# Spatial-reduction attention and a mixture of adapters on one core: a new start (load order, idle products on TensorE, new order list for the first 14 slots)

## The chip, the cores and the metric

The kernel runs on 1 core of one Trainium2 chip. The metric is the device time of one execution in microseconds. Before the change it is 393.75 us, the median of 4 runs (393.65 to 394.62).

## The reference

Queries `q` (4 batches, 12288 tokens each, 128 channels), `kv` (4 batches, 384 x 32 positions, 128 channels) and small weights, all fp32. Each batch pools `kv` by 4 x 4 positions to 768 rows and multiplies them with `w_sr`; the result serves as keys and as values. Softmax attention of all queries over these 768 keys gives `x`, and a mixture of 8 low-rank adapters (2 of 8 by token) adds to it:

```python
kv_pool = kv.reshape(B, H // 4, 4, W // 4, 4, C).mean(axis=(2, 4))
k = v = kv_pool.reshape(B, -1, C) @ w_sr
a = softmax(q @ k.T / sqrt(C));  x = a @ v
logits = x @ w_gate              # the two largest of 8, softmax over the two
out = x + sum over the two: weight * (x @ A[e]) @ B[e]
```

## The kernel before

The 49152 tokens are cut into 96 slots of 512 (24 for each batch; four slots are a query group). For each slot TensorE does three score pairs (two products of 512 columns each, PSUM tile `sg`, two buffers), ScalarE takes the exponential of each pair (`em`, line 252), TensorE multiplies `em` with the values in 24 products of 137 columns (`acc`, one buffer: 128 channels, 8 gate logits, and the row sum), VectorE normalizes (`xn`, lines 264 and 268), and the adapters follow: transposes (`tt_ps`), down product (`h_ps`), gate (`hg`), transposes, up product (`d_ps`), and the sum that goes out (`osb`). The routing (lines 299 to 314) runs on GpSimd, for slots 0 and 1 on VectorE.

The small PSUM tiles share a pool of two buffers (`mb`). All instructions are kept in the order in which they are written for their engine. This order comes from a list of short items that `follow` reads, for the first 14 slots and for the last 24 slots by hand; for slots 14 to 71 `slot(k)` writes it. The items that matter here, with their arguments:

- `sc k r`: score pair r (of 3) of slot k, and its exponential; `at k s`: 6 of the 24 attend products of slot k; `nm k`: its normalization.
- `tq g m E`: query turn, four fp32 transposes of one chunk of query group g and the copy to `qT` on engine E (A is ScalarE, V is VectorE). Groups 0 and 1 are loaded in fp32 and turned like this; later groups are cast to bf16 by a GpSimd DMA (`cast_q`) and read back through a DMA transpose on SP's queue (`lq`, `load_qT`).
- `ad h i`: one of four pair sums of key block h (of 3) of batch 0 on VectorE (line 175): two of the four rows of a pooling window are added. `ky h half`: 8 fp32 transposes ("key turns") that add up in PSUM; then the mean (line 206). `k2 h`: projection of the keys (line 213). `va h`: projection of the values (line 222).
- `cs1`: the GpSimd instruction that reads the last column of query group 1 and thereby holds the two first casts behind that load; `kv b h r`: a load of batch b. `pa` and `pr`: sums on GpSimd and preparation of the next batch.

Ahead of the list stand the loads on SP's queue: query group 0 as one DMA of 1 MB, the 24 pieces of 256 KB of the three key blocks of batch 0, four pieces of query group 1, and the adapters' weights. `w_sr` and `w_gate` come by ScalarE's queue; VectorE and TensorE then make `wext` and its gate part from them.

Of the kernel before, what the change touches and what calls it, by code (L numbers as in the profile page):

```python
# [20 lines left out]
def kernel(  # L21
# [10 lines left out]
    nc = tc.nc  # L32
# [74 lines left out]
    def turn_q(g, m, engine):  # L107
        if g not in qT:
            qT[g] = qpool.tile([P, GT], BF16, tag="qT", name="qT")
        ps = mtile([P, S, P], name="qT_ps")  # L110
        for i in range(S):
            mm(ps[:, i], q_f[g][:, m * S + i], id_f, is_transpose=True,
               start=(i == 0), stop=(i == S - 1))
        o = qT[g][:, m * T:(m + 1) * T].rearrange("p (s t) -> p s t", s=S)
        if engine is nc.scalar:
            keep(nc.scalar.copy(o, ps))
        else:
            keep(nc.vector.tensor_copy(o, ps))
# [6 lines left out]
    load_q(0, 0, GC * S)  # L125
    for h in range(3):
        for r in range(4):
            for x in range(2):
                load_kv(0, h, r, x)
    for m in range(GC):  # L130
        load_q(1, m * S, m * S + S)
    b_f = const.tile([P, C], FP32)
    keep(nc.sync.dma_start(b_f, moe_B.rearrange("e r c -> (e r) c")))
    a_f = const.tile([P, P], FP32)
    keep(nc.sync.dma_start(a_f, moe_A.rearrange("e c r -> c e r")))


    warm = const.tile([P, 1], FP32)
    nc.vector.memset(warm, 0.0)
    keep(nc.scalar.activation(warm, warm, AF.Exp, bias=0.0, scale=1.0))  # L140
    id_f = const.tile([P, P], FP32)
    make_identity(nc, id_f)
    id_bf = const.tile([P, P], BF16)
    nc.vector.tensor_copy(id_bf, id_f)
    wext = const.tile([P, VC], FP32)
    nc.vector.tensor_copy(wext[:, 0:C], w_sr_sb)
    wT_ps = mtile([P, C], name="wT_ps")
    mm(wT_ps, w_sr_sb, id_f, is_transpose=True, start=True, stop=True)
    wT = const.tile([P, C], FP32)
    nc.vector.tensor_copy(wT, wT_ps)  # L150
    w2_ps = mtile([P, E], name="w2_ps")
    mm(w2_ps, wT, w_gate_sb, start=True, stop=True)
    nc.vector.tensor_copy(wext[:, C:VC], w2_ps)


    kfT, vx = {}, {}

    def prepare(b, adder):
# [3 lines left out]
        def pool_step(h, step, lo, hi):  # L162
            t = kvr[b, h]
            if step < 3:
                u, v = t[:, 0].rearrange("p g c -> p (g c)"), t[:, step + 1].rearrange("p g c -> p (g c)")
            else:
                w = 2 * C if step == 3 else C
                u, v = t[:, 0, :, 0:w], t[:, 0, :, w:2 * w]
                keep(adder.tensor_tensor(u, u, v, op=ALU.add))
                return  # L170
            keep(adder.tensor_tensor(u[:, lo:hi], u[:, lo:hi], v[:, lo:hi], op=ALU.add))  # L171

        def pair_step(h, r, x):
            u, v = (kvr[b, h][:, r + i, x] for i in range(2))
            keep(adder.tensor_tensor(u, u, v, op=ALU.add))

        for h in range(3):
            if adder is nc.vector:
                sums.append([lambda h=h, r=r, x=x: pair_step(h, r, x)
                             for r in (0, 2) for x in range(2)])  # L180
                continue
# [5 lines left out]
        def keys(h, half=None):  # L187
            if h == 0 and half != 1:
                st["kpT"] = prep.tile([P, J, P], FP32, tag="kpT", name="kpT")
                kfT[b] = per_b.tile([P, J, P], BF16, tag="kfT", name="kfT")  # L190
            kpT = st["kpT"]
            if half != 1:
                st["ps"] = mtile([P, 2, P], name="kpT_ps")
            ps = st["ps"]
            if adder is nc.vector:
                parts = [(r, i, c) for r in (0, 2) for i in range(2) for c in range(4)]
            else:
                parts = [(0, i, 0) for i in range(2)]
            for n, (r, i, c) in enumerate(parts):
                if half is not None and r // 2 != half:  # L200
                    continue
                mm(ps[:, i], kvr[b, h][:, r, i, c * C:(c + 1) * C], id_f, is_transpose=True,
                   start=(n == 0), stop=(n == len(parts) - 1))
            if half == 0:
                return
            keep(nc.vector.tensor_scalar(kpT[:, 2 * h:2 * h + 2], ps, 1.0 / 16.0, None,
                                         op0=ALU.mult))

        def keys2(h):
            kpT = st["kpT"]  # L210
            ps = mtile([P, 2, P], name="kfT_ps")
            mm(ps, w_sr_sb, kpT[:, 2 * h:2 * h + 2], start=True, stop=True)
            keep(nc.vector.tensor_copy(kfT[b][:, 2 * h:2 * h + 2], ps))  # L213

        def values(h):
# [7 lines left out]
            if adder is not nc.vector:  # L223
                st["vb", h] = prep.tile([P, 2, C], BF16, tag="vb", name="vb")
                keep(nc.vector.tensor_copy(st["vb", h], ps[:, :, 0:C]))
# [8 lines left out]
        for h in range(3):  # L234
            for f in (keys, keys2, values) if adder is nc.vector else (keys, values, turn):
                rest.append(lambda h=h, f=f, **how: f(h, **how))
# [17 lines left out]
    def attend(k, s):  # L254
        b = k // NB
        if k not in acc:
            acc[k] = ps_a.tile([P, S, 256], FP32, tag="acc", name="acc")
        o = acc[k][:, s, 0:VE]
        for j in range(J):
            mm(o, em[k][:, j, s * P:(s + 1) * P], vx[b][:, j], start=(j == 0), stop=(j == J - 1))  # L260
# [11 lines left out]


# [16 lines left out]
    def route(k0):  # L290
        n = size[k0] * S
        eng = nc.gpsimd if k0 > 1 else nc.vector
# [74 lines left out]
    def bank(pool):  # L367
# [20 lines left out]
    def turn_x(k, pool):  # L388
        xT[k] = quad(bank(pool).bitcast(BF16), pool)
        xb = xn[k].bitcast(U16)[:, :, 1::2].bitcast(BF16)  # L390
        for s in range(S):
            mm(xT[k][:, s // 2, s % 2], xb[:, s, 0:C], id_bf, is_transpose=True,
               start=(s % 2 == 0), stop=(s % 2 == 1))

    def copy(engine, o, i):
        keep(nc.scalar.copy(o, i) if engine == "A" else nc.vector.tensor_copy(o, i))  # L396

    def fetch_x(k, engine):
        sb = run.tile([P, S, P], BF16, tag="tt1", name="tt1")
        copy(engine, four(sb), xT[k])  # L400
        xT[k] = sb
# [3 lines left out]
    def hold_h(k, pool):  # L405
        hps[k] = quad(bank(pool).bitcast(BF16), pool)

    def turn_h(k, lo=0, hi=S):
        for s in range(lo, hi):
            mm(hps[k][:, s // 2, s % 2], hg[k][:, s], id_bf, is_transpose=True,  # L410
               start=(s % 2 == 0), stop=(s % 2 == 1))

    def fetch_h(k, lo=0, hi=S, engine="A"):
        if lo == 0:
            hgT[k] = run.tile([P, S, P], BF16, tag="tt1", name="tt1")
        copy(engine, part(four(hgT[k]), lo, hi), part(hps[k], lo, hi))

    def hold_acc(k, pool="sg"):
        acc[k] = bank(pool)
# [3 lines left out]
    def attend_part(k, lo, hi):  # L423
        for s in range(S):
            for j in range(lo, hi):
                mm(acc[k][:, s, 0:VE], em[k][:, j, s * P:(s + 1) * P], vx[k // NB][:, j],
                   start=(j == 0 and s % 2 == 0), stop=(j == J - 1 and s % 2 == 1))

    def down_into(k, pool):
        hp[k] = quad(bank(pool), pool)  # L430
        for s in range(S):
            mm(hp[k][:, s // 2, s % 2], xT[k][:, s], a_bf, start=(s % 2 == 0), stop=(s % 2 == 1))

    def gate_part(k, lo, hi):
        if lo == 0:
# [3 lines left out]
        keep(nc.vector.tensor_tensor(  # L439
            part(four(hg[k]).rearrange("p a b (e r) -> p a (b e) r", e=E), lo, hi),  # L440
            part(four(hp[k]).rearrange("p a b (e r) -> p a (b e) r", e=E), lo, hi),
            part(g4, lo, hi).unsqueeze(3).broadcast_to([P, (hi - lo) // 2, 2 * E, RK]), op=ALU.mult))

    def hold_d(k, pool):
        dp[k] = quad(bank(pool), pool)

    def up_part(k, lo, hi):
        for s in range(lo, hi):
            mm(dp[k][:, s // 2, s % 2], hgT[k][:, s], b_bf, start=(s % 2 == 0), stop=(s % 2 == 1))
# [5 lines left out]
    def add_here(k, lo, hi, queue="SP"):  # L455
        osb = opool.tile([P, S, C], FP32, tag="osb", name="osb")[:, 0:hi - lo]
        keep(nc.vector.tensor_tensor(osb.rearrange("p (a b) c -> p a b c", b=2),
                                     part(four(dp[k]), lo, hi),
                                     part(four(xn[k][:, :, 0:C]), lo, hi), op=ALU.add))
# [57 lines left out]
    def plan(b):  # L517
        if b not in plans:
            plans[b] = prepare(b, nc.gpsimd if b else nc.vector)
# [3 lines left out]
        "tq": lambda g, m, e: turn_q(g, m, nc.scalar if e == "A" else nc.vector),  # L523
        "ad": lambda h, i: plan(0)[0][h][i](),
        "ky": lambda h, half: plan(0)[1][3 * h](half=half),
        "k2": lambda h: plan(0)[1][3 * h + 1](),
        "va": lambda h: plan(0)[1][3 * h + 2](),
        "cs": lambda: first_casts(kvr[0, 2][:, 3, 1, 0:1]),
        "cs1": lambda: first_casts(q_f[1][:, GC * S - 1, 0:1]),
# [10 lines left out]
        "xt": turn_x, "cx": lambda k, e="A": fetch_x(k, e), "hb": hold_h, "ht": turn_h, "ch": fetch_h,  # L540
        "o95": hold_acc, "pt": attend_part, "dn2": down_into, "ge2": gate_part,
# [4 lines left out]
    def follow(order):  # L546
        for item in order.replace("\n", " ").split(";"):
            what, *at = item.split()
# [31 lines left out]
ad 0 0; tq 0 0 A; ad 0 1; ad 0 2; cs1; tq 0 1 A; ad 0 3; ky 0 0; tq 0 2 V; ky 0 1; k2 0; ad 1 0; va  # L580
0; sc 0 0; tq 0 3 A; lq 2; sc 2 0; ad 1 1; ad 1 2; ad 1 3; ky 1 0; sc 1 0; ky 1 1; ad 2 0; sc 3 0;
k2 1; ad 2 1; va 1; sc 3 1; ad 2 2; sc 0 1; ky 2 0; sc 2 1; ad 2 3; kv 1 0 0; ky 2 1; sc 1 1; k2 2;
tq 1 0 V; sc 0 2; va 2; cab; sc 4 2; tq 1 1 V; at 0 2; kv 1 0 1; sc 1 2; at 0 1; sc 4 0; at 0 0; at
# [89 lines left out]
```

## Time and profile before

| | |
|---|---|
| median of 4 runs | 393.75 us |
| profiled execution, its own time | 393.65 us |
| its span, first to last instruction | 391.9 us |
| TensorE busy | 377.0 us (96%) |
| VectorE busy | 324.8 us (83%) |
| ScalarE busy | 298.1 us (76%) |
| GpSimd busy | 204.7 us (52%) |
| DMA | 76.47 MB, mean 195 GB/s |
| chain that ended last | TensorE 93%, VectorE 3%, DMA 1%, issue 1%, ScalarE 1% |

Busy times overlap. A product that is listed with 379 ns for 512 columns is counted until its end; the next one starts earlier, so TensorE's pace is read from the chain of work that ended last, where each piece stands with the time that it adds. The granted clock is given for each stretch of time.

### The profile page before, as it was taken

The page shows a single profiled execution, that of the slowest core. Times are in us where ns is not written, and L with a number is a line of the kernel's source. Part 1 is how long each engine was busy: PE and PEld are TensorE (multiplying, and loading weights), DVE is VectorE, ACT ScalarE, POOL GpSimd, SP SyncE. Part 2 cuts the span into 40 slices and gives each one's busy share as a digit, 9 for nine tenths or more (in the row PEclk, how much of TensorE's full clock was granted, in tenths as well). Part 3 has the DMA queues.
Part 4 walks back from the last instruction along what each step waited for, and adds up shares of the span by engine and source line. Part 5 has one row for each costly group of instructions (what it writes and reads, how often), then busy time and mean ns, then how long its engine had stood idle before and what let it go on. Part 6 is the DMA issues. An engine that isn't in the chain of part 4 may idle for free.

```text
span 391.9 us, 11714 instructions
## 1 busy us (share of the span) xinstructions
PE 377.0 (96%) x4589; PEld 303.2 (77%) x4589; DVE 324.8 (83%) x950; ACT 298.1 (76%) x375; POOL 204.7 (52%) x473
## 2 busy tenths in 40 slices
PE   3999999999999999999999999999999899999994
PEld 2767878888887888888878878888787678878882
DVE  2666768989888889888988888989888888888885
ACT  2378888787688787787777877877787787887883
POOL 0010479998331787777332777867433334444443
PEclk9999999999999999999999999999999999999996
DMA  8998979874696999774599999666645566573213
GB/s 298 372 262 215 215 250 265 237 166 136 143 312 166 292 244 297 194 162 136 112 267 209 300 276 294 159 156 123 155 140 109 160 148 150 152 153 103 82 57 136
DMA packets 71465, 76.47 MB, mean 195 GB/s; under 512 B 49937, under 2 KB 50705, under 8 KB 70929
## 3 DMA queue, kind: packets, MB, share of 16 engines
q1 hardware_dynamic: 70272, 63.98, 56.0%
q0 software_dynamic: 704, 11.54, 16.9%
q8 instruction: 36, 0.59, 0.6%
q10 hardware_dynamic: 432, 0.20, 0.2%
q14 instruction: 21, 0.16, 0.1%
HBM read 50.53 MB, written 36.70 MB: 223 GB/s over the span
## 4 chain that ended last, share of the span: by engine, by line
PE 93%; DVE 3%; DMA 1%; issue 1%; ACT 1%; POOL 0%; ACTq 0%; DVEq 0%; POOLq 0%
PE acc L68 35%; PE sg L68 31%; PE tt_ps L68 10%; PE h_ps L68 5%; PE d_ps L68 5%; PE kpT_ps L68 2%; DMA w_sr_sb<-in_w_sr_dram 1%; PE v_ps L68 1%; PE qT_ps L68 1%; PE kfT_ps L68 1%; DVE tts L335 1%; DVE xn L268 1%; PE tail_ps L68 0%; ACT tt L396 0%; DVE kfT L213 0%
## 5 line engine op out<-in xcount | busy, mean ns | idle before, releaser
L252 ACT ACTIVATE em<-sg 128x1024 f16<-128x1024 f32 x288 | 281.0, 1022 | 76.2 <-PE sg L68 75.5
L68 PE MATMUL sg<-qT,kfT 128*128 128x512 bf16 x576 | 170.4, 379 | 0.2
L68 PE MATMUL acc<-vx,em 128*128 128x137 f16 x2280 | 168.1, 223 | 0.0
L68 PEld LDWEIGHTS <-em 128*128 128x128 f16 x2304 | 146.1, 98 | 3.1 <-DVE xn L268 1.1
L68 PEld LDWEIGHTS <-tts 128*128 128x128 bf16 x740 | 56.1, 98 | 44.0 <-issue 2.8
L171 POOL TENSOR_TENSOR kvr<-kvr 128x512 f32<-128x512 f32 x54 | 67.5, 1274 | 15.1 <-DVE hg L349 15.1
L268 DVE TENSOR_TENSOR xn<-acc,rinv 128x544 f32<-128x544 f32 x95 | 68.8, 724 | 3.3
L349 DVE TENSOR_TENSOR hg<-h_ps,gw 128x512 bf16<-128x512 f32 x93 | 64.2, 690 | 7.0 <-PE h_ps L68 0.2
L335 DVE COPY tts<-tt_ps 128x1024 bf16<-128x1024 bf16 (+1 forms) x93 | 61.5, 662 | 2.3 <-PE tt_ps L68 1.5
L362 DVE TENSOR_TENSOR osb<-d_ps,xn 128x512 f32<-128x512 f32 x89 | 61.2, 690 | 0.0
L299 POOL TENSOR_TENSOR over<-xn,srt 128x64 f32<-128x64 f32 (+1 forms) x116 | 30.3, 283 | 55.4 <-DVE srt L286 55.4
L313 POOL TENSOR_TENSOR gw<-th,over 128x64 f32<-128x64 f32 (+1 forms) x58 | 17.0, 293 | 68.8 <-ACT th L311 68.6
L68 PEld LDWEIGHTS <-kfT 128*128 128x128 bf16 x576 | 45.5, 98 | 2.5 <-DVE kfT L213 0.8
L264 DVE RECIPROCAL rinv<-acc 128x4 f32<-128x4 f32 x95 | 17.4, 183 | 35.4 <-PE acc L68 34.8
L68 PEld LDWEIGHTS <-xn 128*128 128x128 bf16 x384 | 28.9, 98 | 20.0 <-DVE xn L268 0.4
L68 PE MATMUL d_ps<-b_bf,tts 128*128 128x128 bf16 x364 | 35.2, 219 | 1.6 <-DVE tts L335 1.1
L68 PE MATMUL h_ps<-a_bf,tts 128*128 128x128 bf16 x372 | 36.0, 219 | 0.3 <-ACT tts L333 0.3
L68 PE MATMUL tt_ps<-id_bf,xn 128*128 128x128 bf16 x372 | 35.8, 219 | 0.0
L68 PE MATMUL tt_ps<-id_bf,hg 128*128 128x128 bf16 x368 | 35.6, 219 | 0.0
L286 DVE MAX8 srt<-xn 128x8 f32<-128x8 f32 x380 | 34.3, 153 | 0.0
L68 PEld LDWEIGHTS <-hg 128*128 128x128 bf16 x384 | 26.0, 98 | 1.9 <-issue 0.6
L305 POOL TENSOR_SCALAR over<-over 128x64 f32<-128x64 f32 (+1 forms) x58 | 19.4, 335 | 5.3
(83 smaller groups left out, 210.1 us busy)
## 6 DMA issues: line engine op xcount, KB each, us to landing
out_dram<-osb SPq DMA_DIRECT2D x94, 256.0 KB, 3.4
kvr<-in_kv_dram SPq DMA_DIRECT2D x36, 512.0 KB, 5.9
qbf<-in_q_dram POOLq DMA_DIRECT2D x22, 512.0 KB, 6.2
kvr<-in_kv_dram SPq DMA_DIRECT2D x24, 256.0 KB, 5.1
qf<-in_q_dram SPq DMA_DIRECT2D x1, 1024.0 KB, 5.1
qf<-in_q_dram SPq DMA_DIRECT2D x4, 256.0 KB, 5.2
out_dram<-osb SPq DMA_DIRECT2D x3, 128.0 KB, 2.1
qT<-qbf SPq DMA_TRANSPOSE x22, 5.3
```

Source lines behind the costliest of these rows:

```text
L68: return keep(nc.tensor.matmul(*a, **k))
L171: keep(adder.tensor_tensor(u[:, lo:hi], u[:, lo:hi], v[:, lo:hi], op=ALU.add))
L252: keep(nc.scalar.activation(em[k][:, 2 * r:2 * r + 2], ps, AF.Exp, bias=0.0, scale=scale))
L264: keep(nc.vector.reciprocal(ri, acc[k][:, :, VC]))
L268: keep(nc.vector.tensor_tensor(x, acc[k][:, :, 0:VC], ri.unsqueeze(2).broadcast_to([P, S, VC]), op=ALU.mult))
L286: keep(nc.vector.max(srt[k0][:, m, s], xn[k][:, s, C:VC]))
L299: keep(eng.tensor_tensor(d, lg, so[:, :, i].unsqueeze(2).broadcast_to([P, n, 8]), op=ALU.subtract))
L305: keep(eng.tensor_scalar(mask, mask, 0.0, None, op0=ALU.is_ge))
L313: keep(eng.tensor_tensor(w[:, 0:n], th, mask, op=ALU.mult))
L335: keep(nc.vector.tensor_copy(sb[:, lo:hi], ps[:, lo:hi]))
L349: keep(nc.vector.tensor_tensor(hg[k].rearrange("p s (e r) -> p (s e) r", e=E), hp[k].rearrange("p s (e r) -> p (s e) r", e=E), gw[k0][:, m ...
L362: keep(nc.vector.tensor_tensor(osb, dp[k], xn[k][:, :, 0:C], op=ALU.add))
```

## The change

- **Loads.** SP's queue gets a new order: rows 1 and 0 of key block 0, a chunk of query group 1, rows 3 and 2, the two halves of query group 0, then blocks 1 and 2, then the other three chunks of query group 1. Most rows of keys are now loaded whole (512 KB) instead of in halves. The total is the same.
- **Spin.** VectorE fills a bf16 tile `idle` with zeros; TensorE runs 11 products of 512 columns on it into a PSUM tile that nobody reads.
- **The start of batch 0.** `prepare` loses its VectorE variant. Pair sums, key turns, mean, projections and copies become items of their own (`ad`, `ky`, `kb`, `kc`, `k2`, `va`) that name PSUM pool and engine. A pair that isn't summed on VectorE is turned row by row (`turn_k`), so that PSUM adds all four rows.
- **The list for slots 0 to 13** is new. It has attend items by key block (`pt k lo hi`), normalization by halves (`nh`), and adapter steps in single transposes (`xt`, `cx`, `ht`, `ch`). Slots 14 and on, and the tail, keep their order.
- **Routing** of slots 0 and 1 moves to GpSimd.
- **Casts.** `cs` watches the last column of query group 1, as `cs1` did.
- **Waits.** `use` declares that instructions on different PSUM banks of one tile don't depend on each other, for the tiles of `acc` and `sg` that are used in halves.

```diff
-    load_q(0, 0, GC * S)
-    for h in range(3):
-        for r in range(4):
-            for x in range(2):
-                load_kv(0, h, r, x)
-    for m in range(GC):
-        load_q(1, m * S, m * S + S)
+    for item in """
+lkv 0 1 -; lkv 0 0 -; lf 1 1 2; lkv 0 3 -; lkv 0 2 -; lf 0 0 2; lf 0 2 4; lkv 1 2 -; lkv 1 3 -; lkv
+1 0 -; lkv 1 1 1; lkv 1 1 0; lkv 2 3 -; lkv 2 2 -; lkv 2 0 0; lkv 2 1 0; lkv 2 0 1; lkv 2 1 1; lf 1
+2 3; lf 1 0 1; lf 1 3 4; lab
+""".replace("\n", " ").split(";"):
...
+    idle = const.tile([P, T], BF16)
+    keep(nc.vector.memset(idle, 0.0))
...
+    def spin(n):
+        ps = mtile([P, T], name="spin_ps")
+        for i in range(n):
+            mm(ps, idle[:, 0:P], idle, start=True, stop=True)
+
+    spin(11)
...
+    def use(key, lo, hi, inst):
+        if key not in split:
+            return
+        mine = set(range(lo // 2, (hi + 1) // 2))
+        for other, theirs in users.setdefault(key, []):
+            if not mine & theirs:
+                tc.declare_no_dep(inst.ins, other.ins, reason="other PSUM bank")
+        users[key].append((inst, mine))
...
+    def turn_k(h, half, x):
...
+        rows = [2 * half] if (h, 2 * half, x) in summed else [2 * half, 2 * half + 1]
+        todo[h] -= 1
+        for r in rows:
+            for c in range(4):
+                mm(first_ps[h][:, x], kvr[0, h][:, r, x, c * C:(c + 1) * C], id_f, is_transpose=True,
+                   start=(h not in seen), stop=(todo[h] == 0 and r == rows[-1] and c == 3))
+                seen[h] = True
...
-        eng = nc.gpsimd if k0 > 1 else nc.vector
+        eng = nc.gpsimd
...
-        "cs": lambda: first_casts(kvr[0, 2][:, 3, 1, 0:1]),
-        "cs1": lambda: first_casts(q_f[1][:, GC * S - 1, 0:1]),
+        "cs": lambda w: first_casts(q_f[1][:, 15, 0:1]),
...
-ad 0 0; tq 0 0 A; ad 0 1; ad 0 2; cs1; tq 0 1 A; ad 0 3; ky 0 0; tq 0 2 V; ky 0 1; k2 0; ad 1 0; va
-0; sc 0 0; tq 0 3 A; lq 2; sc 2 0; ad 1 1; ad 1 2; ad 1 3; ky 1 0; sc 1 0; ky 1 1; ad 2 0; sc 3 0;
-k2 1; ad 2 1; va 1; sc 3 1; ad 2 2; sc 0 1; ky 2 0; sc 2 1; ad 2 3; kv 1 0 0; ky 2 1; sc 1 1; k2 2;
-tq 1 0 V; sc 0 2; va 2; cab; sc 4 2; tq 1 1 V; at 0 2; kv 1 0 1; sc 1 2; at 0 1; sc 4 0; at 0 0; at
-0 3; sc 2 2; nm 0; tq 1 2 V; sc 5 1; kv 1 0 2; at 1 3; at 1 0; at 1 2; at 1 1; sc 6 2; nm 1; tq 1 3
...
+kb 1 mb; kb 0 sg; init; ad 0 2; ky 0 0 1; ky 0 0 0; tq 1 1 V mb; db 1 sg; ky 0 1 1; cs k; xb 3 mb;
+ky 0 1 0; kb 2 mb; kc 0 A; tq 0 0 A acc; tq 0 1 A sg; k2 0 sg A; lq 2; tq 0 2 V mb; tq 0 3 V mb; ad
+1 2; va 0 acc A; sc 5 0; kv 1 0 0; sc 0 0; ad 1 1; ky 1 1 1; ky 1 1 0; sc 1 0; sc 3 0; ky 1 0 0; ky
+1 0 1; ad 2 3; pt 0 0 2; ad 2 2; kc 1 A; ad 2 0; k2 1 mb A; ad 2 1; sc 2 0; va 1 mb V; sc 5 1; ky 2
+1 1; sc 1 1; ky 2 1 0; sc 3 1; ky 2 0 0; sc 0 1; ky 2 0 1; kv 1 0 1; kv 1 0 2; kc 2 V; tq 1 2 A mb;
+sc 2 1; k2 2 mb V; sc 6 1; va 2 mb V; kv 1 0 3; sc 0 2; tq 1 3 V mb; pt 0 2 4; sc 3 2; pt 0 4 6; sc
+1 2; tq 1 0 A mb; xb 1 mb; sc 2 2; nm 0; pt 1 0 2; hb 0 mb; pt 1 2 4; pt 1 4 6; sc 4 1; nh 1 0; nh 1
...
```

## The prediction

> **What bounds the kernel now.** I read the stages first (busy time in stretches of 10 us), then the chain of work that ended last, then the timeline of the first 30 us. Columns of the stages: stretch, length, busy us (instructions) of each engine, granted clock, DMA share, GB/s.
>
> ```profile
> 0.00:10.00 10.00, 3.48 (x15) 2.99 (x16) 2.21 (x7) 2.66 (x4) 0.69 (x6) 1.00 0.82 299
> 10.00:20.00 10.00, 9.34 (x54) 7.41 (x53) 6.54 (x13) 3.76 (x5) 0.00 (x0) 1.00 1.03 374
> 20.00:30.00 10.00, 9.78 (x77) 7.12 (x76) 5.93 (x13) 7.76 (x9) 1.38 (x3) 1.00 0.84 240
> 30.00:40.00 10.00, 10.00 (x118) 7.93 (x116) 7.28 (x34) 8.98 (x11) 0.00 (x0) 1.00 0.89 243
> ```
>
> From 30 us on TensorE is never idle; its first 30 us are not full, and until 20 us the DMA engines are (share 1.03). The chain (start, length, what) gives TensorE's pace and the losses:
>
> ```profile
> 0.72 5.28 DMA w_sr_sb<-in_w_sr_dram
> 7.56 1.80 PE qT_ps L68 x8
> 9.36 1.79 PE kpT_ps L68 x8
> 11.16 0.85 PE qT_ps L68 x4
> 12.01 1.73 PE kpT_ps L68 x8
> 13.77 0.44 DVE kpT L206
> 14.25 0.71 PE kfT_ps L68 x2
> 14.98 0.44 DVE kfT L213
> 15.47 0.61 PE sg L68 x2
> 16.94 0.87 PE kpT_ps L68 x8
> 26.51 0.46 PE v_ps L68 x4
> 28.20 0.43 PE sg L68 x2
> 29.42 0.72 PE acc L68 x12
> ```
>
> An fp32 turn costs 0.22 us before 13.3 us and 0.109 after (0.87/8): TensorE starts slow and doubles its rate at 13.3 us. At full rate a score pair costs 0.43, a query turn (4) 0.44, an attend product 0.06, a key projection 0.43, a value projection 0.46. After 30.14 us the chain is TensorE alone until the tail, and from order slot 14 on TensorE's instructions are the same list in both kernels. So the change is worth what it does to TensorE's progress in the first 30 us, plus whatever it stalls later. Three more things are read from the timeline: when data lands, and when ScalarE starts.
>
> ```profile
> 12.02 0.69 DVE L175 TENSOR_TENSOR kvr<-kvr 128x512 f32<-128x512 f32 x1 [0.78 <-DMA kvr<-in_kv_dram]
> 16.11 1.02 ACT L252 ACTIVATE em<-sg 128x1024 f16<-128x1024 f32 x1 [6.12 <-PE sg L68]
> 25.35 0.18 POOL L507 COPY late<-qf 128x1 f32<-128x1 f32 x1 [24.05 <-DMA qf<-in_q_dram]
> 28.67 3.88 ACT L252 ACTIVATE em<-sg 128x1024 f16<-128x1024 f32 x4 [0.18 <-PE sg L68]
> ```
>
> The last piece of key block 0 lands at 12.0 us (3.15 MB so far), the last query piece at 25.3 (8.39 MB): 0.394 MB/us. An exponential costs 0.97 us in a chain (3.88/4).
>
> **Where before stands.** At 30.14 us it has issued 48 key turns (5.2), 6 query turns (2.6), 3 projections of keys and values (1.3 + 1.4), 12 score pairs (5.2) and 24 attends (1.4): 17.1 us of work at full rate from a start at 7.4. So 5.6 us are lost: 2.8 in 27 turns at half rate, the rest in the three waits for mean and projection copies (13.77, 14.98 and their like at blocks 1 and 2) and for a row sum.
>
> **The change, part by part.**
>
> *Spin.* Eleven 512-column products on zeros; at half rate twice the 0.216 of a score product, 4.7 us. VectorE's memset of warm ends at 0.86; that of the zeros is not in the trace (between 0.06, a small memset, and 0.42, a 256-column copy); I take 0.3, so it spins from 1.2 to 5.9. The weights that the first real product needs land at 6.0, so the spin costs nothing; with the longer memset 0.1. What it buys is the clock. In the trace the rate doubled 5.9 us after the steady stream began (7.42 to 13.3), 7.2 us after the first product (6.14). Counted from 1.2 this gives 7.1 to 8.4 if the gaps around 6 to 7 us don't break the count, and 13.3 again if they do. I take 7.1, since the gaps (0.2 and 0.5 us) are short beside 4.7. The Trainium skill (TensorE: Matmul & The Clock Gate, section "What's actually happening") says that the clock is raised after a busy window of about 3.4 us that runs freely, regardless of the kernel's start. By that page 4.7 us of spin hold a whole window in only (4.7 - 3.4)/3.4 = 38% of the phases, an estimate, which speaks against the change: in the others the clock could stay low past 10 us, and the sum would move from the forecast toward the low-clock rival below. The 5.9 us of the trace fit a window missed and the next one taken.
>
> *Loads.* The same 8.4 MB, keys of block 0 ahead of most queries, and most in rows of 4 KB, whose packets took 159 ns where those of 2 KB took 84: 5% quicker per byte. Counting bytes at the trace's rate with that bonus: block 0 complete at 9.1 instead of 12.0 (2.4 instead of 3.15 MB), second half of query group 0 at 12.4, rows 2 and 3 of block 1 at 15.0, all of block 1 at 17.6 (before 17.5), block 2 at 22.8 (before 22.7), last query piece at 24.9.
>
> *Row sums to turns.* Blocks 0 and 1 keep one and two of four pair sums; TensorE turns the rest unsummed: 28 + 24 + 16 = 68 turns instead of 48, +20 x 0.109 = +2.2 us, on the path. VectorE is rid of 5 x 0.69.
>
> *Order of the start, walked through with these durations (clock up).* Weights until 7.2. Sixteen turns to 8.9, query turn of chunk 1 to 9.3, rows 2 and 3 (landed 9.1) with 8 turns to 10.2, the summed 4 to 10.6. The mean, now on ScalarE (0.4), is done at 11.3; query turns 0 and 1 cover it to 11.5. Projection to 12.0; query turn 2 waits for its data at 12.4 (lost 0.45 with the projection's lead); turns and values to 13.7. First score pair 13.7 instead of 15.47; the exponentials start at 14.4 instead of 16.1. Then losses: rows 2 and 3 of block 1 at 15.0 (0.4); its last half row at 17.6 (0.4); the projection of block 1 behind ScalarE's mean, which queues behind two exponentials, and its copy (0.45); score pairs that wait for one of the two score buffers (0.6 in five places, by 0.97 per exponential); lead of the last projection (0.1); score pair "6 1" behind the query copy on ScalarE (0.4). On VectorE the four sums of block 2 wait in order for data until 22.8, and the value copy of block 1 sits behind them to 24.0; the next TensorE step that needs it comes after 28 us, its buffer is wanted at 24.9: free. Sum of losses 2.8.
>
> At the end of attend "0" (all 24) after has 68 turns (7.4), 7 query turns (3.1), the projections (2.7), 13 score pairs (5.6) and 24 attends (1.4): 20.2 us. 7.2 + 20.2 + 2.8 = 30.2 us, with one score pair and one query turn (0.87) more than before had at 30.14. Gain 0.87 - 0.06 = 0.8 us.
>
> *Slots 0 to 13.* TensorE work is equal. The single acc buffer changes hands after 0.18 + 0.72 us of VectorE and some 0.25 of signalling: 1.15. The new list puts 1.2 to 1.5 us of other products there in each slot I looked at, so nothing; if one in three misses by 0.2, +0.8. ScalarE has about 29 exponentials (28), 6 copies (3.5), small ones (2.3) for 36 us: 33.8, no bound, but only 2 us of air.
>
> *Two routings moved to GpSimd.* 6 small operations at 0.22 to 0.29 each, 1.5 us per slot, 3.0 in all, less one 1.27 add: into its idle 15.1 us ahead of 41.83. Key sums of batch 1, behind them on that queue, ended at 65.1 and were needed at 70.1: 5 us of cover.
>
> *Casts.* They watch the last query piece, as before did: 24.9 for 25.35, and the DMA transposes and the loads of batch 1 queued behind them on SP follow. Nothing.
>
> *Tail.* Finer waits between PSUM banks: VectorE's two 0.38 us halves at 384.28 may start after half of a 0.40 us product group. 0 to -0.15; I take -0.1.
>
> Sum: -0.8 - 0.1 = -0.9. On the profiled execution (393.65; span 391.9 and 1.75 around it, 0.1 under the median of 393.75): 392.75, or 392.7 rounded toward the shorter packets. A measurement here can tell about 0.2% (0.8 us) from no change, so the forecast lies just past that bound.
>
> **The rivals.**
>
> *The clock stays low until 13 us* (slower). For it: the rate needed 5.9 us of steady stream, the spin has 4.7, and two gaps follow; against it: 4.7 of stream and 0.4 of weights lie in the 5.9 before 7.1. Also the case in which products on zeros raise nothing. Price: 28 turns at +0.104 is 2.9 us up to the first score pair (16.7); 0.8 of it is absorbed in the waits for block 1. ScalarE's chain starts as late and keeps it. -0.9 + 2.1 = +1.2: 394.85. It decides if the rate doubles later than about 10.6 us (each us of low clock costs half, 0.9 + 0.8 absorbed).
>
> *ScalarE takes the place* (no change). Means, projection and value copies and three query copies of the first slots move to it, among exponentials; if its copies from PSUM come one exponential later at blocks 1 and 2 (0.97), the gain is gone: 393.7. For it: it is busy 7.76 of 10 in 20 to 30 us and now more. It also stands for a clock that rises at 9 to 11 us.
>
> *Data comes sooner* (faster by more): without the three landing waits (0.4 + 0.4 + 0.4) 391.5. Against it: the DMA share is 1.03 already.
>
> **How the numbers follow.** Forecast 0.50, four fifths of it past the bound; low clock 0.22; ScalarE 0.18; sooner data 0.10. Faster 0.40 + 0.10 = 0.50; no change 0.10 + 0.18 = 0.28; slower 0.22. The range runs from sooner data to low clock, 391.5 to 394.9; the forecast's own is 392.2 to 393.3 (the +0.5 of missed acc handovers, -0.5 of landings).
>
> **What would show it.** Right: turns at 0.109 us from about 7 us, first score pair near 13.7, exponentials from 14.4, no TensorE loss after 30 us, slot 14's first score pair (67.6 before) at 66.8. Wrong: 0.22 us turns after 10 us; waits of score products on exponentials beyond 0.6 us in all; TensorE waiting on VectorE's normalization after 30 us.

## The result and the profile after

The changed kernel takes 393.24 us (median of 33 runs, 392.82 to 394.24), the kernel before 393.74 us (53 runs, 393.16 to 394.62): ratio 0.9987, 95% interval 0.9982 to 0.9992. It is faster, by 0.5 us where 1.05 were forecast, so the gain is 0.13% and does not pass the 0.2% (0.8 us) that the forecast hoped to pass. The times split in a way that the forecast did not expect:

| median, us | time | span | outside the span |
|---|---|---|---|
| before (74 runs of the later comparisons) | 393.8 | 392.0 | 1.79 |
| after (34 runs) | 393.2 | 391.1 | 2.09 |

The span is 0.9 us shorter, which is the forecast's sum. But 0.3 us come back outside it.

Stages of the profile after (393.01 us, span 390.9; columns as before the change: stretch, length, busy us of TensorE, its weight loads, VectorE, ScalarE, GpSimd, then clock, DMA share, GB/s):

```profile
0.00:10.00 10.00, 7.71 (x34) 4.10 (x34) 1.15 (x6) 1.49 (x2) 0.69 (x6) 1.00 0.80 272
10.00:20.00 10.00, 9.75 (x77) 8.30 (x78) 4.00 (x7) 6.27 (x10) 0.00 (x0) 1.00 1.03 410
20.00:30.00 10.00, 9.51 (x71) 6.77 (x69) 5.10 (x10) 9.15 (x11) 1.38 (x3) 1.00 0.84 231
30.00:40.00 10.00, 10.00 (x123) 7.98 (x122) 6.72 (x34) 8.96 (x12) 2.31 (x10) 1.00 0.93 239
```

TensorE is busier in the first 10 us (7.71 for 3.48, 4.7 of it on zeros), ScalarE between 10 and 20 us (6.27 for 3.76); from 30 us on TensorE is full in both. The timeline of after shows the steps:

```profile
1.21 4.87 PE L68 MATMUL spin_ps<-idle 128*128 128x512 bf16 x11 [1.21 <-DVE idle L141]
2.59 0.23 DVE L157 COPY wext<-w_sr_sb 128x128 f32<-128x128 f32 x1 [1.44 <-DMA w_sr_sb<-in_w_sr_dram]
5.88 0.42 PE L68 MATMUL wT_ps<-id_f,w_sr_sb 128*128 128x128 f32 x1
6.92 1.95 PE L68 MATMUL sg<-id_f,kvr 128*128 128x128 f32 x16
10.17 1.53 PE L68 MATMUL sg<-id_f,kvr 128*128 128x128 f32 x12 [0.86 <-DMA kvr<-in_kv_dram]
14.18 1.03 PE L68 MATMUL sg<-qT,kfT 128*128 128x512 bf16 x4
14.81 1.94 ACT L319 ACTIVATE em<-sg 128x1024 f16<-128x1024 f32 x2
23.45 0.66 PE L68 MATMUL tail_ps<-id_f,kvr 128*128 128x128 f32 x4 [0.34 <-DVE kvr L195]
24.69 0.66 PE L68 MATMUL tail_ps<-id_f,kvr 128*128 128x128 f32 x4 [0.15 <-DVE kvr L195]
```

Sixteen turns take 1.95 us from 6.92 on, 0.12 each, half of the 0.22 that they took there before. The clock rose at 6.19 us (13.44 before). The first score pair is at 14.18 (15.47), the first exponential at 14.81 (16.11). The first turn of batch 1 (`pr 1 0`), after which both lists are equal, comes at 69.02 us for 70.11 (first line before, second line after): the start has gained 1.09 us.

```profile
70.11 0.39 PE L68 MATMUL kpT_ps<-id_f,kvr 128*128 128x128 f32 x2
69.02 0.39 PE L68 MATMUL kpT_ps<-id_f,kvr 128*128 128x128 f32 x2
```

This milestone is used below for all kernels. The chain of work that ended last (start, length, what) now begins with key loads; its last line here ends the attends of slot 0:

```profile
1.44 4.89 DMA kvr<-in_kv_dram
6.35 10.03 DMA kvr<-in_kv_dram
16.40 7.45 DMA kvr<-in_kv_dram
23.94 0.70 DVE kvr L195
24.69 1.09 PE tail_ps L68 x8
29.32 0.55 PE acc L68 x8
```

It says that the start is bound by the last key piece, which lands at 23.85 us, 1.2 later than in before (22.67), and by its sum. Fifteen of its 16 shares, one for each DMA engine, had landed by 22.75; the sixteenth is 1.1 us late, and in every load since the one that ended at 21.99 us one share is as late. Just before, from 19.68 us on, a DMA engine fetched 16 KB of TensorE's program, for 0.88 us. In before this fetch comes at 26.3, past the key loads, and no single share stands out. Whether the lag costs anything is tested below.

### The profile page after: what moved, and what is told of

It is laid out like the page before. It is cut to its first block, busy times and chain, and to the rows that moved or that the text cites. A ratio compares the mean times of both kernels' runs of the same rounds, so it can differ in the third digit from the quotient of the medians.

```text
span 390.9 us, 11774 instructions
## 1 busy us (share of the span) xinstructions
PE 379.5 (97%) x4620; PEld 303.6 (78%) x4620; DVE 318.6 (81%) x939; ACT 300.5 (77%) x383; POOL 206.5 (53%) x484
## 4 chain that ended last, share of the span: by engine, by line
PE 89%; DMA 6%; DVE 2%; ACT 1%; issue 1%; SPq 0%; POOL 0%; ACTq 0%; DVEq 0%; POOLq 0%
PE acc L68 35%; PE sg L68 30%; PE tt_ps L68 10%; DMA kvr<-in_kv_dram 6%; PE h_ps L68 5%; PE d_ps L68 5%; PE tail_ps L68 2%; PE v_ps L68 1%; DVE tts L416 1%; PE kpT_ps L68 1%; DVE xn L337 1%; ACT tt L177 0%; ACT tts L414 0%; PE kfT_ps L68 0%; DVE osb L551 0%
## 5 line engine op out<-in xcount | busy, mean ns | idle before, releaser
L68 PEld LDWEIGHTS <-tts 128*128 128x128 bf16 x708 | 53.7, 98 | 43.2 <-issue 2.8
L337 DVE TENSOR_TENSOR xn<-acc,rinv 128x544 f32<-128x544 f32 x92 | 66.6, 724 | 3.4 <-DVE rinv L333 0.3
L380 POOL TENSOR_TENSOR over<-xn,srt 128x64 f32<-128x64 f32 (+1 forms) x120 | 31.2, 282 | 63.6 <-DVE srt L367 63.6
L430 DVE TENSOR_TENSOR hg<-h_ps,gw 128x512 bf16<-128x512 f32 x85 | 58.8, 691 | 6.7
L416 DVE COPY tts<-tt_ps 128x1024 bf16<-128x1024 bf16 (+1 forms) x87 | 59.1, 679 | 1.3 <-ACT em L319 0.7
L443 DVE TENSOR_TENSOR osb<-d_ps,xn 128x512 f32<-128x512 f32 x85 | 58.4, 691 | 0.0
L68 PE MATMUL tt_ps<-id_bf,xn 128*128 128x128 bf16 x360 | 34.8, 219 | 0.0
L68 PE MATMUL d_ps<-b_bf,tts 128*128 128x128 bf16 x336 | 32.4, 219 | 1.6 <-DVE tts L416 1.1
L68 PE MATMUL h_ps<-a_bf,tts 128*128 128x128 bf16 x348 | 33.7, 219 | 0.3 <-ACT tts L414 0.3
L68 PE MATMUL tt_ps<-id_bf,hg 128*128 128x128 bf16 x348 | 33.5, 219 | 0.0
```

What stands on the lines that cost most here:

```text
L68: return keep(nc.tensor.matmul(*a, **k))
L337: keep(nc.vector.tensor_tensor(x, acc[k][:, :, 0:VC], ri.unsqueeze(2).broadcast_to([P, S, VC]), op=ALU.mult))
L380: keep(eng.tensor_tensor(d, lg, so[:, :, i].unsqueeze(2).broadcast_to([P, n, 8]), op=ALU.subtract))
L416: keep(nc.vector.tensor_copy(sb[:, lo:hi], ps[:, lo:hi]))
L430: keep(nc.vector.tensor_tensor(hg[k].rearrange("p s (e r) -> p (s e) r", e=E), hp[k].rearrange("p s (e r) -> p (s e) r", e=E), gw[k0][:, m ...
L443: keep(nc.vector.tensor_tensor(osb, dp[k], xn[k][:, :, 0:C], op=ALU.add))
```

## The experiments

All times are medians; before was run beside each (393.8, 393.5, 393.8 and 393.95 us in the four comparisons).

**e1_no_spin**: after without the spin.

```diff
-    spin(11)
```

> The changed kernel without the 11 products on zeros. Clock theory (the prediction's): the rate doubles only after some 6 us of steady turns, between 10 and 14 us; about 20 to 28 turns cost 0.213 instead of 0.109 us, 2 to 3 us up to the first score pair, 0.8 to 1.5 of it absorbed in waits for keys; so 0.7 to 1.8 us slower than the changed kernel, which is 0.2 to 1.3 slower than before. Data theory (rival: the first 24 us only wait for the last key piece, which lands at 23.85 us in the changed kernel): within 0.3 us of the changed kernel, and the pair of weight products starts near 2.6 us, when the weights land, instead of 5.9.

Measured: 393.43 us (12 runs), ratio 0.9987 (0.9977 to 0.9997), span 391.35, `pr 1 0` at 69.54. The clock rose at 12.18 us. TensorE's waits until 30 us (who waited for what: us, times, longest):

```profile
PE wT_ps L68 <- DMA w_sr_sb<-in_w_sr_dram: 2.6, 1, 2.6
PE w_ps L68 <- DMA w_gate_sb<-in_moe_w_gate_dram: 2.5, 1, 2.5
PE sg L68 <- DMA kvr<-in_kv_dram: 0.4, 1, 0.4
```

So with a clock that is low for 6 us longer the median span is 0.25 us above that of after, and that is not clear of the scatter (390.8 to 391.8 here, 390.8 to 392.2 in after; the ratios to before are both 0.9987). This is what the data theory gave. The weight products start at 2.64 us, and the 0.4 us in the list is a wait for rows 1 and 0, at 6.63 us. For rows 2 and 3, landed at 10.19, TensorE does not wait at all: its slow turns last until 10.95. With the spin it waits 0.9 us for them.

**e2_before_spin**: before with the spin alone.

```diff
+    idle = const.tile([P, T], BF16)
+    keep(nc.vector.memset(idle, 0.0))
...
+    spin_ps = mtile([P, T], name="spin_ps")
+    for i in range(11):
+        mm(spin_ps, idle[:, 0:P], idle, start=True, stop=True)
```

> The kernel before, with the 11 products on zeros in front of its first real product and nothing else changed. Clock theory: the 27 half-rate turns (2.8 us lost) run at full rate, but the last row sum of block 0 waits for data until 12.7 us, so the first score pair comes at 14.8 instead of 15.5 and the kernel gains 0.4 to 0.7 us, all or more than the whole change. Data theory: what is gained at 15 us is lost again at the landings of blocks 1 and 2 (17.5 and 22.7 us); 0 to 0.2 us.

Measured: 393.68 us (12 runs), ratio 0.9997 (0.9987 to 1.0006), `pr 1 0` at 69.97. The clock rose at 5.84 us, and the time it saved went into other waits of TensorE:

```profile
PE kpT_ps L68 <- DVE kvr L180: 2.2, 3, 0.9
PE kfT_ps L68 <- DVE kpT L211: 0.8, 2, 0.5
```

The spin alone gains nothing that can be measured, as the data theory had it: sums and landings come no sooner.

**e3_full_sums**: after with all pair sums on VectorE, 48 key turns instead of 68.

```diff
-kb 1 mb; kb 0 sg; init; ad 0 2; ky 0 0 1; ky 0 0 0; ...
+kb 1 mb; kb 0 sg; init; ad 0 1; ky 0 0 1; ad 0 0; ky 0 0 0; tq 1 1 V mb; db 1 sg; ad 0 3; ...
```

> The changed kernel with all pair sums on VectorE again, 48 turns instead of 68. TensorE theory (the prediction's term of 2.2 us on the path): up to 2.2 us faster than the changed kernel. Data theory: the 20 turns fill time in which TensorE waits for data or ScalarE, so they cost little; blocks 0 and 1 come 0.4 to 0.5 us later behind the sums; but TensorE has issued 40 instructions fewer, so its 16 KB program fetch, which in the changed kernel starts at 19.7 us after 226 instructions and holds one DMA engine's share of the last four key pieces back by 1.1 us, comes near 22 us: last key piece near 22.8 instead of 23.85, and the kernel is 0.3 to 0.9 us faster.

Measured: 393.94 us (12 runs, 392.83 to 396.21), ratio 1.0006 (0.999 to 1.0023), `pr 1 0` at 69.64. The last key piece landed at 22.89 us, the fetch coming at 22.56. But TensorE now waits 1.47 and 1.38 us for sums of block 0, and in the first of these gaps the clock falls back (columns as in the stages, clock last but two):

```profile
4.00:7.00 3.00, 1.53 (x8) 0.73 (x6) 0.70 (x3) 0.00 (x0) 0.00 (x0) 1.00 1.03 338
7.00:10.00 3.00, 2.50 (x12) 2.42 (x12) 1.05 (x2) 0.00 (x0) 0.00 (x0) 0.55 1.02 411
10.00:13.00 3.00, 1.62 (x12) 1.11 (x11) 1.89 (x3) 0.00 (x0) 0.00 (x0) 0.88 1.02 384
```

Its runs differ with the mean clock: the three at 0.992 or more have spans of 390.8 to 391.4, no better than after (391.1), the one at 0.982 has 394.1. So taking the 20 added turns out wins nothing back, even with the clock up: while row sums make TensorE wait, the turns keep it busy. They are no loss of 2.2 us.

**e4_old_loads**: after with the load order of before.

```diff
-lkv 0 1 -; lkv 0 0 -; lf 1 1 2; lkv 0 3 -; ...
+lf 0 0 4; lkv 0 0 0; lkv 0 0 1; lkv 0 1 0; ... ; lf 1 0 1; lf 1 1 2; lf 1 2 3; lf 1 3 4; lab
```

> The changed kernel with the loads in the order and the sizes of the kernel before (query group 0 first, keys in halves). Prediction's terms: block 0 complete at 12.0 instead of 10.1 us, so the first score pair comes about 1.5 us later; 0.7 to 1.5 us slower. Data theory: the last key piece, not the first, decides, and it comes 0.25 MB earlier in this order but in slower pieces, so within 0.4 us of the changed kernel.

Measured: 408.66 us (5 runs), ratio 1.0366 (1.0344 to 1.0388). One wait makes it up:

```profile
PE tail_ps L68 <- DMA qf<-in_q_dram: 14.2, 1, 14.2
```

The new list turns a chunk of query group 1 before rows 2 and 3 of block 0; in the old order that chunk is among the last loads, and TensorE takes its instructions in order. The edit was badly chosen: it prices this dependence, not the order of keys and queries. For that order g2_queries_first is the nearer test.

**f1_loads_only**: before with the load order of after (the same lines, the other way round).

> The kernel before with only the load list of the kernel after (whole rows, keys of block 0 ahead of most queries); order list, sums and routing stay. Theory 1 (loads and order list only pay together): block 0 is complete near 10.1 us instead of 12.0, but the old list begins with two turns of query group 0, whose first half lands only near 11 and whose second near 12.4, so the first score pair comes at 15.5 to 17 us, turn 'pr 1 0' of batch 1 at 70.1 to 71.2, and the time is 393.7 to 394.8. Rival (keys first are the gain): first score pair near 14.2, 'pr 1 0' near 69.0, 393.0 to 393.3. For the 0.3 us that the kernel after spends outside its span (2.08 against 1.78): if the loads cause it, it is 2.08 here; if GpSimd's program does, 1.78.

Measured: 397.5 us (4 runs), ratio 1.0097 (1.0082 to 1.0112), `pr 1 0` at 74.84; outside the span 1.75. Worse than theory 1 had it: the old list begins with query turns, which now wait for their data, and the clock, without turns to raise it, rises at 17.22 us.

```profile
PE qT_ps L68 <- DMA qf<-in_q_dram: 5.5, 1, 5.5
PE wT_ps L68 <- DMA w_sr_sb<-in_w_sr_dram: 2.7, 1, 2.7
PE w_ps L68 <- DMA w_gate_sb<-in_moe_w_gate_dram: 2.4, 1, 2.4
```

Load order and list gain together. The loads alone lose 4 us against the kernel before; the list alone loses 15, nearly all of it in the one wait of e4.

**g2_queries_first**: after with three query loads (0.75 MB) ahead of the keys.

```diff
-lkv 0 1 -; lkv 0 0 -; lf 1 1 2; lkv 0 3 -; lkv 0 2 -; lf 0 0 2; lf 0 2 4;
+lf 1 1 2; lf 0 0 2; lf 0 2 4; lkv 0 1 -; lkv 0 0 -; lkv 0 3 -; lkv 0 2 -;
```

> The kernel after with three query loads (0.75 MB: the chunk of group 1 and both halves of group 0) ahead of the keys of block 0; all else as in after. Theory (block 0's landing sets the first score pair): rows 2 and 3 of block 0 land near 12.3 us instead of 10.1, the turns of queries and keys come in the list's order, the first score pair at 15.8 to 16.4 instead of 14.2, 'pr 1 0' at 69.9 to 70.9 instead of 69.02, 393.9 to 395.0. Rival (the last key piece and ScalarE set the pace anyway): first score pair near 16, but 'pr 1 0' within 0.4 of 69.02 and 393.1 to 393.6.

Measured: 396.85 us (4 runs), ratio 1.0076 (1.006 to 1.0091), `pr 1 0` at 72.31: the direction of the theory, twice its size. The timeline shows why:

```profile
10.38 3.67 PE L68 MATMUL sg<-id_f,kvr 128*128 128x128 f32 x16 [2.88 <-DMA kvr<-in_kv_dram]
18.29 1.03 PE L68 MATMUL sg<-qT,kfT 128*128 128x512 bf16 x4
```

After spin and weights TensorE waits 2.88 us for keys, until 10.38, then turns at half rate (0.22 each; the clock rose at 13.95), and the first score pair comes at 18.29. With this list, keys first are worth 3.5 us of span (394.65 against 391.1). Part of that is the low clock, which no run takes apart from the order.

**f2_route_dve**: after with the routing of slots 0 and 1 back on VectorE.

```diff
-        eng = nc.gpsimd
+        eng = nc.gpsimd if k0 > 1 else nc.vector
```

> The kernel after with the routing of slots 0 and 1 back on VectorE, 12 instructions fewer on GpSimd. Theory (program fetch): GpSimd's longer program crosses one more 8 KB piece, fetched 1.5 us after the last recorded instruction; without it the time outside the span is 1.78 to 1.82 instead of 2.08, and the median 392.85 to 393.0, if VectorE's 12 small operations (some 1.5 us per slot) lie beside TensorE's work. Rival 1 (the loads or the order list cause it): 2.08 outside, 393.2. Rival 2 (VectorE is short of air in slots 0 to 3): outside 1.8, but 'pr 1 0' 0.3 or more later than 69.02, and 393.2 or more.

Measured: 394.94 us (5 runs), ratio 1.0033 (1.002 to 1.0045); span 393.2, outside the span 1.77. Both halves count. The 0.3 us outside are gone, as the theory said; and the span is 2.1 us longer than that of after (rival 2). Timeline of this kernel:

```profile
44.73 0.24 ACT L392 ACTIVATE th<-over 128x32 f32<-128x32 f32 x1
45.01 1.07 DVE L394 TENSOR_TENSOR gw<-th,over 128x32 f32<-128x32 f32 x1 [2.29 <-ACT th L392]
46.70 0.40 PE L68 MATMUL h_ps<-a_bf,tt 128*128 128x128 bf16 x4 [1.12 <-DVE tt L177]
```

VectorE takes its instructions in order and stands 2.29 us at the gate of slot 1, because the tanh that it needs is queued behind exponentials on ScalarE; a copy and a normalization behind it are late, and TensorE waits for them. In after the same waits lie on GpSimd (window 38 to 60 us), where nothing urgent is queued behind them; TensorE waits for nothing from 30 to 70 us:

```profile
POOL gw L394 <- ACT th L392: 3.1, 2, 2.0
```

**f5_before_pool**: the same line in before, the other way.

```diff
-        eng = nc.gpsimd if k0 > 1 else nc.vector
+        eng = nc.gpsimd
```

> The kernel before with one line changed: the routing of slots 0 and 1 goes to GpSimd instead of VectorE, 12 more instructions on GpSimd and 12 fewer on VectorE. Theory (program fetch): a second 8 KB fetch 1.5 us after the last recorded instruction, and 2.05 to 2.12 us outside the span instead of 1.78. Rival (the loads or the order list): 1.78. The span itself stays within 391.5 to 392.3.

Measured (one run): 393.54 us, span 391.6, outside 1.94, and an 8 KB program fetch 1.52 us after the end of the span. The direction is that of the theory, the size half of it (0.15 for 0.3). One run cannot show more.

**g1_fewer_pool**: after with 18 fewer instructions on GpSimd.

```diff
+            if step < 3 and b > 1:
+                if lo:
+                    return
+                hi = 1024
```

> The kernel after with 18 fewer instructions on GpSimd: in batches 2 and 3 each pair of 512-column adds of the row sums (three pairs per key block) is one add of 1024 columns; the routing stays on GpSimd. Theory (program fetch): the extra 8 KB fetch 1.5 us after the last recorded instruction goes, the time outside the span is 1.75 to 1.82 instead of 2.08 with the span unchanged at 391.1, and the median is 392.9. Rival 1 (the routing itself, not GpSimd's instruction count, decides): 2.08 outside, 393.2. Rival 2 (adds of twice the length hold up gates on GpSimd and then TensorE): span 0.3 or more longer.

Measured: 392.67 us (9 runs, 392.51 to 393.53), ratio 0.9976 (0.9967 to 0.9986); span 390.9, outside 1.80, and no fetch after the span. The theory's numbers hold in the medians. Rival 2 shows too, in the profiled run, which took 393.53 us: GpSimd is in an add of 1024 columns (2.36 us), the tanh of a gate waits for GpSimd, exponentials stand behind the tanh, and TensorE waits for one of them:

```profile
137.76 0.26 ACT L396 ACTIVATE th<-over 128x64 f32<-128x64 f32 x1 [1.24 <-POOL over L389]
138.98 0.59 PE L68 MATMUL sg<-qT,kfT 128*128 128x512 bf16 x2 [0.39 <-ACT em L323]
```

From there on its score products are 0.56 us later against `pr 1 0` than those of after. Three of the nine runs took 393.37 to 393.53 us, the others 392.51 to 392.72; whether the other two long ones lost their time in the same place, no trace shows.

Over all kernels the time outside the span goes with the number of GpSimd's recorded instructions: 561 to 568 (six kernels, with either load order, with and without spin) give 1.75 to 1.80, 578 gives 1.94, 579 (five kernels) 2.07 to 2.10, 580 (two) 2.23 and 2.24. From 578 on, an 8 KB fetch comes 1.0 to 1.7 us after the last recorded instruction; below, only f1_loads_only has one past its span, at 0.5 us, at no cost. Why one more instruction there costs some 0.15 us stays open. The median of this kernel is 1.1 us under before. Against after, with which it was not run in one comparison, its median is 0.6 us lower, but with three runs of nine above after's median that it is faster is not shown.

**f3_late_fetch and g3_late_fetch**: two tries to move the 16 KB fetch of TensorE's program past the key loads, by fewer TensorE instructions ahead of them. Common to both:

```diff
-    idle = const.tile([P, T], BF16)
+    idle = const.tile([P, T], FP32)
...
-    spin(11)
+    spin(3)
...
-1 0 1; ad 2 3; pt 0 0 2; ad 2 2; ...
+... ky 2 0 0; sc 0 1; pt 0 0 2; ky 2 0 1; ...
```

Both also have one more fp32 product on zeros, f3_late_fetch between key turns, g3_late_fetch ahead of them. f3_late_fetch sums all of blocks 0 and 1 on VectorE. g3_late_fetch spins with two products, adds only the sums of the first rows of block 0, and moves `va 1` behind most of block 2's turns.

> The kernel after with fewer TensorE instructions before the last key piece: spin of 3 fp32 products instead of 11 bf16 ones (12 instead of 22 records), one fp32 product on zeros as filler ahead of the turns of rows 2 and 3, all pair sums of blocks 0 and 1 on VectorE (24 turns fewer, less one block's that were summed already: 20), and the first 8 attend products of slot 0 moved behind most of block 2's turns. Theory (the 16 KB fetch of TensorE's program at 19.7 us holds one DMA engine back by 1 us): the fetch comes at 22.3 us or later, the last key piece lands at 22.7 to 23.0 instead of 23.85, TensorE's two waits on sums of block 2 (0.8 us) shrink to 0.3 or less, 'pr 1 0' at 68.2 to 68.7 instead of 69.02, the time 392.4 to 392.9. Rival (ScalarE's chain of exponentials, which begins at 14.8 us, sets the pace through 30 us): the last key piece does land at 22.9, but 'pr 1 0' stays at 68.9 to 69.3 and the time at 393.1 to 393.5. If the clock falls back in the gap near 9 us as with all sums before, first score pair near 15.4 and 393.9.

Measured: 395.23 us (5 runs), ratio 1.0045 (1.0031 to 1.0058), `pr 1 0` at 71.13. The last key piece landed at 22.91, but the weight copies stood behind sums on VectorE, TensorE idled 1.75 us at 6.8, and the clock fell back from 9.72 to 13.14. It tells nothing on the lag.

> A second try at fewer TensorE instructions before the last key piece, without what held the first one up: 2 fp32 products of spin, then the products of the weights, one more fp32 product on zeros, and the sums of the first rows of block 0 behind the weight copies on VectorE; block 1's sums as in after; the first 8 attend products of slot 0 and the value projection of block 1 behind most of block 2's turns. Theory (the 16 KB fetch costs its 1 us of lag): fetch at 22.3 us or later, last key piece at 22.7 to 23.0, first score pair near 14.2, 'pr 1 0' at 68.2 to 68.8, 392.4 to 392.9. Rival (ScalarE's chain from 14.8 us sets the pace through 30 us): last key piece near 22.9, 'pr 1 0' at 68.9 to 69.4, 393.1 to 393.6. If the clock falls back in the gap before 10 us: first score pair past 15, 393.6 or more.

Measured: 393.40 us (11 runs), ratio 0.9987 (0.9976 to 0.9998), span 391.3, `pr 1 0` at 69.52. Here the start kept its pace (first score pair at 14.27, clock up at 4.88 for good), the fetch came at 24.59, and the last key piece at 22.82, 1.0 us earlier than in after:

```profile
22.91 0.69 DVE L195 TENSOR_TENSOR kvr<-kvr 128x512 f32<-128x512 f32 x1 [0.58 <-DMA kvr<-in_kv_dram]
24.42 0.68 PE L68 MATMUL tail_ps<-wext,kpT 128*128 128x136 f32 x4
24.93 0.60 PE L68 MATMUL tail_ps<-id_f,kvr 128*128 128x128 f32 x4
```

The sum ends at 23.6, and the turns that need it still start at 24.93 (24.69 in after): TensorE is busy with other work until then. So the lag is real, and it goes with the fetch: the fetch comes at 19.6 to 21.9 us where the last key piece lands at 23.85 to 24.1 (after, e1, f2, g1), and at 22.5 or later where that piece lands by 23.0 (before, e2, e3, e4, f1, f3, f5, g2, g3). Only g4 below does not fit this. But with the lag moved away nothing was gained: the time is the rival's (393.1 to 393.6). What holds TensorE there is its own queue, with the products that were moved to this place, rather than ScalarE's chain alone, which the rival named. So this run does not show that the lag was free in after. There its price is at most the 0.49 us that TensorE waits for the two sums (0.34 and 0.15).

**g4_keys_all_first**: g1_fewer_pool with all keys of block 0 ahead of every query load, and the first score pairs ahead of two query turns; one query copy (`tq 0 1`) also goes from ScalarE to VectorE.

```diff
-lkv 0 1 -; lkv 0 0 -; lf 1 1 2; lkv 0 3 -; lkv 0 2 -; lf 0 0 2; lf 0 2 4;
+lkv 0 1 -; lkv 0 0 -; lkv 0 3 -; lkv 0 2 -; lf 0 0 2; lf 1 1 2; lf 0 2 4;
...
-ky 0 0 0; tq 1 1 V mb; ... k2 0 sg A; lq 2; tq 0 2 V mb; tq 0 3 V mb; ad 1 2; va 0 acc A; sc 5 0; sc 0 0; ...
+ky 0 0 0; ... k2 0 sg A; lq 2; tq 1 1 V mb; va 0 acc A; sc 0 0; sc 1 0; tq 0 2 V mb; tq 0 3 V mb; ad 1 2; sc 5 0; ...
```

> The kernel of g1_fewer_pool, and in its start all of block 0's keys ahead of every query load, the turn of query chunk 1 of group 1 moved behind block 0's key projection, and the first score pairs (slots 0 and 1, then 5, 3, 2) ahead of the turns of query chunks 2 and 3. Theory 1 (block 0's landing and the first exponential set the start): rows 2 and 3 of block 0 land at 9.3 to 9.5 us instead of 10.1, first score pair at 12.8 to 13.4 instead of 14.2, 'pr 1 0' at 68.0 to 68.7 instead of 69.0 to 69.3, 391.9 to 392.4. Rival (the last key piece at 23.8 and its sum at 24.6 hold the rest back): first score pair as early, but TensorE's waits at block 2 grow from 0.8 to 1.5 us or more, 'pr 1 0' at 68.9 to 69.3, and 392.5 to 392.8. The time outside the span is 1.75 to 1.82 in both.

Measured: 393.44 us (12 runs), ratio 0.999 (0.9976 to 1.0004), `pr 1 0` at 69.90; outside 1.80. Neither theory's numbers hold.

```profile
9.99 1.53 PE L68 MATMUL sg<-id_f,kvr 128*128 128x128 f32 x12 [1.44 <-DMA kvr<-in_kv_dram]
14.07 1.03 PE L68 MATMUL sg<-qT,kfT 128*128 128x512 bf16 x3
```

Rows 2 and 3 landed at 9.95, not at 9.4: the first DMA engine had its share at 8.23 and thirteen of the 16 by 9.05, the other three at 9.44 to 9.95. To the end of the loads the last share stays about 2 us behind the first (22.53 to 24.56 for the last key piece). No program fetch lies before it; its cause is open. The first score pair came only 0.1 us earlier than in after, and TensorE lost 1.0 us more between there and `pr 1 0`.

## Why the prediction was right, and where it was not

- **The start's sum held.** The turns start at 6.92 (forecast 7.2), all attends of slot 0 are done at 29.87 by the chain (29.32 + 0.55; forecast 30.2, and 30.14 in before by the same reading). Less 20.2 us of work and 6.92, the losses are 2.75 us (forecast 2.8). The gain at batch 1's first turn is 1.09 us in the profiles (forecast 0.8), and 0.9 in the median spans (forecast 0.9).
- **Some of that is luck: single terms in it were off and cancelled.** Rows 2 and 3 of block 0 landed at 10.12, not 9.1. Most of this is a slip of the sum: the 1.05 MB behind them take 2.7 us at its 0.394 MB/us, and from its own 12.4 that gives 9.7. Its next landings were within 0.25 (12.63 for 12.4, 15.12 for 15.0, 17.62 for 17.6). The late rows took the first score pair from 13.7 to 14.18, and 0.8 us fewer were lost from there to the end of slot 0's attends than forecast. The last key piece was 1.05 late, after the program fetch, which the sum did not know. The +2.2 us "on the path" for 20 more turns is TensorE's time, but e3 shows that summing instead does not save it.
- **What the 0.9 us are made of** is shown for the whole change alone. The loads alone lose 4 us (f1), the routing back on VectorE loses 2.1 (f2), all row sums back lose 0.75 of span (e3, with the clock's fall in it), and the spin cannot be told from nothing (e1, e2).
- **The spin and the clock.** The spin ran from 1.21 to 5.88, as forecast. Its premise that `w_sr` lands at 6.0 did not hold with the new loads: it landed at 2.57 (2.50 in e1), yet the turns begin only 0.3 us later than without the spin (6.63 in e1), as the keys land at 6.3. The clock rose at 6.19 for a forecast of 7.1. The rival "low clock" was priced at +2.1 us for a rise at 13 us; e1 rises at 12.18 and loses 0.25 or nothing. The price let only 0.8 of the 2.9 us of slow turns fall into waits; more did: the first score pair of e1 is 1.3 us later than that of after (15.51 for 14.18), where the rival had 3.0, and `pr 1 0` 0.5.
- **The clock's windows.** By the Trainium skill (TensorE: Matmul & The Clock Gate, section "What's actually happening") the window runs freely, and that agrees: in before the rise and the fall lie 372.05 us apart, 109 stretches of 3.41 us; in e3 the clock is up for one such stretch (3.88 to 7.29), then down for one, and over the 14 profiles the first boundary of this grid lies anywhere from 0.15 to 3.37 us after the start. The estimate of 38% that the forecast drew from it asked for a whole window of spin, and was too strict: with a spin the clock rose between 3.9 and 6.8 us in nine of ten profiles (g2 is the tenth), in six of the nine after a stretch that was full, in e3 after a window that was filled only from 1.21 to 3.88 us, 78%.
- **"Nothing" for the routing hid two things.** GpSimd's cover was judged rightly, but it was not asked what the move takes off VectorE: with the new list, 2.1 us of span (f2). And the longer GpSimd program goes with 0.3 us more after the span.
- **The failed step is the last line of the sum:** "393.65; span 391.9 and 1.75 around it". The time around the span was taken as a constant and rose by 0.30 us, with GpSimd's instruction count, as f2 and g1 show by taking instructions out in two different places. That is most of what separates a gain of 0.9 from 0.5; the last 0.1 is within the scatter of the medians.
- **No loss after 30 us** was right: TensorE waits for nothing from 30 to 70 us, and the last score pair still comes 1.09 us earlier (376.32 for 377.41).
- **The tail** (-0.1) gained more than forecast, and more was lost behind it. From the last score product to the end of VectorE's last sum, before takes 11.18 us and after 10.53. Half of the difference goes with the clock, which fell at 385.49 in before and at 388.48 in after. Among the profiles where it fell at most 1.4 us before that end, the old list takes 10.86 to 10.97 (e2, f1, f5) and the new one 10.53 to 10.65 (after, e1, e4, f3, g1 to g4). So the tail itself gained 0.3. But from there to the end of the span it takes 3.06 us in before and 3.85 in after: the last store lands 2.29 us after its issue for 1.89, and the span ends 1.53 us after this landing for 1.15. In all profiles it is 3.06 to 3.33 with the old list and 3.34 to 3.85 with the new. So of the 1.09 us 0.94 are left. Between SP's last wait (389.56) and its next instruction (389.94) lies a gap that before has not; its cause was not tried.
- **Casts**: nothing, as forecast. The last query piece landed at 25.77 (24.9 forecast, 25.30 before), and TensorE waited for nothing behind them.
- **The other rivals** did not happen: no data came sooner, and ScalarE's copies delayed TensorE by less than the 1 us that was priced.

## What to carry to other kernels

An order of loads and an order of instructions are one design: with in-order engines, either alone lost time here (4 us for the loads, 15 for the list, nearly all of it in one wait), and both together, with the routing moved, gained 0.9 us of span. A wait that cannot be avoided belongs on the queue with nothing urgent behind it. And when the expected gain is below 1 us, split the measured time into span and rest for every run: the rest moves too, here by 0.3 us with a dozen instructions on a side engine. Taking 18 out gave the lowest median of this study, but longer ones in their place held up a gate in one profiled run.

## What was not expected of the hardware

- A chain that begins with a late landing is no proof that the landing costs all of its lateness: moved 1 us earlier, with other products in its place, the turns that need it started no sooner (24.93 for 24.69), and TensorE's own queue held them.
- One 16 KB fetch of TensorE's program, with the DMA engines under full load, took 0.88 us, and after it one engine's share of each following load landed 1.0 to 1.2 us after the others'. Shares 1.5 to 2 us apart occur without a fetch too (g4 from 8 us on, before from 13 us on), with several engines late, and their cause is open.
- The clock of TensorE falls again within one window of about 3.4 us: in e3 (3.88 to 7.29) and f3 (6.31 to 9.72) it was active for less than half of the window; over one that was active for 55% (e2, 9.25 to 12.66) it stayed up. What raises it is less clear: a window filled to 78% did (e3), the first two of g2 (0.30 to 7.13), filled to some 73% and 80%, did not, nor did one of before (6.61 to 10.02) that was filled to some 90%.
